# W_out read in rows of 2 KB, w1 - w2 in four parts, and a new order for tile 0's output blocks in a one-core FFT filter with a max-out layer

## The chip, the cores and the metric

One core of one Trainium2 chip runs the whole program in one launch. The metric is the device time of one execution in microseconds (us). TensorE does the matmuls and transposes, VectorE, ScalarE and GpSimd the element-wise work, and SyncE (SP) and GpSimd issue the DMAs. GpSimd's DMAs are the ones that turn fp32 in DRAM into bf16 in SBUF on the way.

## The reference

Each of 8 batch elements has 3072 rows of 256 channels. Every channel is filtered in the frequency domain along the rows, and each filtered row then goes through two matrices, a maximum and an output matrix:

```python
X = np.fft.rfft(x, axis=1)
F = (filt_r + 1j * filt_i)[None, :, :]
y = np.fft.irfft(X * F, n=3072, axis=1)      # 8 x 3072 x 256
h1 = y @ w1                                   # 256 -> 1024
h2 = y @ w2                                   # 256 -> 1024
out = np.maximum(h1, h2) @ w_out              # 1024 -> 256, fp32
```

## The kernel before

**The transform.** 3072 is split into 96 x 32, and the transform is done as matmuls with bf16 tables: 96-point stages (`f1` or `s1` forward, `s4` inverse), 32-point stages with twiddles (`s2` forward, `s3` inverse), and `product` with the filter between them. Between the stages the data has to change its layout. Batch element 0 changes it by transposes on the chip (`s1t`, `t1`, `s3t`, `t2`), the others through two scratch tensors in DRAM: `ad` after the forward 96-point stage, read back as `bt`, and `zd` after the inverse 32-point stage, read back as `zr`. Element 1 goes through `f1`, whose 16 blocks write `ad` in pairs (SP), and `f1_read`, which reads `bt` in two halves (SP). From element 2 on, `load_xf` brings two halves of x into one of three XF buffers (SP), `fold` forms their sum and difference (GpSimd), and `s1` follows.

**The max-out layer.** The maximum is rewritten: max(h1, h2) = relu(y (w1 - w2)) + y w2. With Wd = w1 - w2, Wo = w_out and M = w2 w_out, a row's output is relu(y Wd) Wo + y M. The work goes over 64 tiles of 384 rows, 8 to a batch element. `s4(tt)` makes the transposed y of a tile. `moe_h(tt, j)` gives the j-th of eight blocks of 128 hidden columns: two matmuls into a tile `ph` of the PSUM pool `ps` (six slots), and a relu into `gt` on VectorE or ScalarE. `moe_o(tt, k0, k1)` runs matmuls k0 to k1 of the tile's 30: three output blocks c of 128 rows, each a sum of ten matmuls, eight with Wo and two with M. Blocks are numbered q = 3 tt + c, and two of them share one of the two buffers `po` of the pool `pso`; after the second, VectorE copies the pair to `ot`, and GpSimd issues their two writes to DRAM.

**The order.** It is written out by hand; the engines keep it, and only semaphores let one wait for another. After the opening (tables, element 0's transform, the weights), a loop runs over the tiles in steps, eight to a tile and 64 to a batch element:

```python
for j in range(8):
    step = 8 * i + j
    if tt < 8 * B:
        moe_h(tt, j)
    for fn, a in mid.get((b, step), ()):
        fn(*a)
    if tt > 0:
        n = 3 if j in (3, 7) else 4
        moe_o(tt - 1, k, k + n)
        k += n
    for fn, a in todo.get((b, step), ()):
        fn(*a)
    if j == (4 if i < 7 else 6) and tt + 1 < 8 * B:
        s4(tt + 1)
```

So tile 0's output blocks run during tile 1, from step 8 on. `plan` puts other work at a step: the rest of element 0 (`t2`), element 1's `f1` blocks and `f1_read` (`plan_f1`), and for each later element the loads, folds and "visits" (`plan_f2`). A visit is one sixth of the 32-point stages; visit 0 of element 1, the first to use `bt`, stands at step 24.

**The weights.** `load_w` brings w1 and w2 as fp32 into one tile `WS`, in two halves of 512 hidden columns each (four DMAs of SP, lines 281 and 282). `prep_wd` (line 292, GpSimd) subtracts one half. `cast_w2` (line 285, VectorE) makes `w2b`, the bf16 w2, in four pieces. `prep_t` transposes it (line 299) and ScalarE copies it to `w2T`; `prep_m` (line 306) multiplies it with Wo into M. `load_wo` (line 288) brings w_out with one DMA of GpSimd. On GpSimd's queue the opening ends with two loads of x for element 1, `prep_wd(0)`, `load_wo`, a last load of x, `prep_wd(1)` and `table_ct`. `spin` issues matmuls whose results are not used.

Of the kernel before, what the change touches and what calls it, by code (L numbers as in the profile page):

```python
# [8 lines left out]
FP32 = mybir.dt.float32  # L9
BF16 = mybir.dt.bfloat16  # L10
AF = mybir.ActivationFunctionType
OP = mybir.AluOpType
# [3 lines left out]
D = 256  # L16
# [10 lines left out]
def kernel(  # L27
# [15 lines left out]
    V, S, G, TE = nc.vector, nc.scalar, nc.gpsimd, nc.tensor  # L43
# [8 lines left out]
    Wd = const.tile([128, 2, HID], BF16)  # L52
    Wo = const.tile([128, 8, D], BF16)
# [5 lines left out]
    w2b = const.tile([128, 2, HID], BF16)  # L59
# [9 lines left out]
    pso = ctx.enter_context(tc.tile_pool(name="pso", bufs=2, space=bass.MemoryType.PSUM))  # L69
# [8 lines left out]
    def x_tile(b, c):  # L78
        if c % 2 == 0:
            xb[b] = xpool.tile([128, 8, D], BF16, tag="xb", name="xb")  # L80
        return xb[b][:, 4 * (c % 2):4 * (c % 2) + 4]

    def load_x(b, c, n):
        for k in range(c, c + n):
            xb[b, k] = x_tile(b, k)[0:NP]
        src = x[b].rearrange("(p m) d -> p m d", m=NM)
        m0 = 4 * (c % 2)
        G.dma_start(out=xb[b][0:NP, m0:m0 + 4 * n], in_=src[:, 4 * c:4 * c + 4 * n, :])  # L88
# [98 lines left out]
    def table_ct():  # L187
        G.memset(CT, 0.0)
        for g in range(2):
            G.tensor_copy(CT[64 * g:64 * g + 48, :, 0:48].rearrange("p s (u r) -> p s u r", r=2),  # L190
                          C1[0:48].rearrange("p (u s r) -> p s u r", s=2, r=2))
# [85 lines left out]
    w1f, w2f = WS[:, 0:2], WS[:, 2:4]  # L277
# [4 lines left out]
        nc.sync.dma_start(out=w2f[:, :, js], in_=moe_w2.rearrange("(c p) j -> p c j", p=128)[:, :, js])  # L282

    def cast_w2(h, c):
        V.tensor_copy(w2b[:, c, 512 * h:512 * h + 512], w2f[:, c, 512 * h:512 * h + 512])

    def load_wo():
        G.dma_start(out=Wo, in_=moe_w_out.rearrange("(c p) j -> p c j", p=128))

    def prep_wd(h, engine):  # L290
        js = slice(512 * h, 512 * h + 512)
        engine.tensor_tensor(Wd[:, :, js], w1f[:, :, js], w2f[:, :, js], OP.subtract)  # L292

    def prep_t(jp):
        pt = ps.tile([128, 4, D], BF16, tag="ps", name="pt")
# [126 lines left out]
    def s4(tt):  # L422
        b, i = divmod(tt, 8)
        y_ = ypool.tile([128, 2, 384], BF16, tag="yt", name="y_")
        for dc in range(2):
            py = ps.tile([128, 4, NP], FP32, tag="ps", name="py")
            for m in range(4):
                TE.matmul(py[:, m], zr[b][:, 4 * i + m, 128 * dc:128 * dc + 128], G1, start=True, stop=True)  # L428
            o_ = y_[:, dc].rearrange("p (t m) -> p t m", m=4)
            i_ = py.rearrange("p m t -> p t m")  # L430
            if dc == 0:
                S.activation(o_, i_, AF.Copy, scale=1.0 / 1536.0)
            else:
                V.tensor_scalar(o_, i_, 1.0 / 1536.0, None, OP.mult)
        yt[tt] = y_
# [18 lines left out]
    po = {}  # L454
    ot = {}

    def out_block(tt, c):
        b, i = divmod(tt, 8)
        dst = out[b * N:(b + 1) * N].rearrange("(c p i m) d -> c i p (m d)", c=3, p=32, i=8)[c, i]
        E = G if tt < 8 * B - 2 else nc.sync  # L460
        E.dma_start(out=dst, in_=ot[tt // 2][:, 3 * (tt % 2) + c])  # L461

    def moe_o(tt, k0, k1):
        y_, g_ = yt[tt], gt[tt]
        for k in range(k0, k1):
            c, e = divmod(k, 10)
            n = (e + 2) % 10 if tt == 0 else e
            q = 3 * tt + c
            blk = slice(128 * c, 128 * c + 128)
            if e == 0 and (q % 2 == 0 or q == 24 * B - 1):  # L470
                po[0] = pso.tile([128, 2, D], FP32, tag="po", name="po")
            p_ = po[0][:, q % 2]
            if n < 2:
                TE.matmul(p_, y_[:, n, blk], M[:, n], start=(e == 0), stop=(e == 9))  # L474
            else:
                TE.matmul(p_, g_[:, n - 2, blk], Wo[:, n - 2], start=(e == 0), stop=(e == 9))  # L476
            if e == 9 and q >= 24 * B - 2:
                e = q % 6
                if q % 2 == 0:
                    S.activation(ot[tt // 2][:, e], p_, AF.Copy)  # L480
                else:
                    V.tensor_copy(ot[tt // 2][:, e], p_)
                out_block(tt, c)
            elif e == 9 and q % 2 == 1:
                if q % 6 == 1:
                    ot[tt // 2] = opool.tile([128, 6, D], FP32, tag="ot", name="ot")
                e = q % 6
                V.tensor_copy(ot[tt // 2][:, e - 1:e + 1], po[0])  # L488
                for qq in (q - 1, q):
                    out_block(qq // 3, qq % 3)  # L490

# [48 lines left out]
    def t2(c, engines):  # L540
        if c == 0:
            zr[0] = zrpool.tile([96, NM, D], BF16, tag="zr", name="zr")
        n = 4 // len(engines)
        for k, engine in enumerate(engines):
            pr = ps.tile([96, n, D], BF16, tag="ps", name="pr")
            m0 = 4 * c + n * k
            for m in range(n):
                for dc in range(2):
                    TE.transpose(pr[:, m, 128 * dc:128 * dc + 128], zT[:, dc, m0 + m].rearrange("p u q -> p (u q)"),  # L549
                                 I128)  # L550
            if engine is V:
                V.tensor_copy(zr[0][:, m0:m0 + n], pr)  # L552
            else:
                S.activation(zr[0][:, m0:m0 + n], pr, AF.Copy)

    def spin(n):
        for _ in range(n):
            pd = ps.tile([128, 512], FP32, tag="ps", name="pd")
            TE.matmul(pd, W1[:, 0:128], W1, start=True, stop=True)  # L559
# [73 lines left out]
    for c in (2, 4):  # L633
        load_x(1, c, 2)
    prep_wd(0, G)
    load_wo()
    load_x(1, 6, 2)
    prep_wd(1, G)
    table_ct()
    setup.close()  # L640
    apool = ctx.enter_context(tc.tile_pool(name="apool", bufs=3))
# [4 lines left out]
    f1(1, 0, S)  # L646
    spin(1)
    t2(0, (V, S))
    spin(2)
    s4(0)  # L650
    spin(2)


# [2 lines left out]
    def plan(b, step, fn, *a):  # L656
        todo.setdefault((b + step // 64, step % 64), []).append((fn, a))

    def plan_f1(b, nb, steps, read):
        for c, n in zip(range(1, 16), steps):  # L660
            plan(b, n, f1, nb, c, S if c % 2 == 0 else V)
        plan(b, read, f1_read, nb)
# [3 lines left out]
    def plan_f2(b, steps, quads, xs, folds):  # L666
        for n, st in enumerate(steps):
            mid.setdefault((b, st), []).append((visit, (b + 1, n, quads[n])))
        plan(b, steps[3] + 3, z_read, b + 1, 0)
        plan(b, steps[6] + 3, z_read, b + 1, 1)  # L670
        if b + 2 < B:
            for c in range(8):
                plan(b, xs[c], load_xf, b + 2, c)
                plan(b, folds[c], fold, b + 2, c)
            plan(b, steps[-1] + (6 if b else 11), s1_read, b + 2)

    plan(0, 2, t2, 1, (V,))
    for h in range(2):
        for c in range(2):
            plan(0, 3 + 2 * h + c, cast_w2, h, c)  # L680
    plan(0, 5, prep_t, 0)
    plan(0, 7, prep_t, 1)
    plan(0, 8, prep_m)
    for c in range(2, 8):
        plan(0, 8 * (c - 2) + 8, t2, c, (V,))
    plan_f1(0, 1, (0, 1, 1, 3, 4, 4, 5, 6, 6, 7, 8, 10, 11, 11, 12), 13)
    plan_f2(0, (24, 28, 31, 35, 38, 42, 46), ((0,), (1,), (2,), (3,), (4,), (5,), (6, 7)),
            (6, 10, 14, 18, 21, 25, 29, 33), (14, 18, 21, 25, 28, 32, 36, 40))
    for b in range(1, B - 1):
        plan_f2(b, (7, 14, 18, 24, 31, 38, 42) if b > 1 else (14, 18, 24, 30, 34, 39, 42), ((0, 1), (2,), (3,), (4,), (5,), (6,), (7,)),  # L690
                range(-32, 32, 8) if b > 1 else range(-25, 31, 7), range(-22, 42, 8) if b > 1 else range(-15, 41, 7))
# [1 line left out]
    for tt in range(8 * B + 1):  # L693
        b, i = divmod(tt, 8)
        k = 0
# [14 lines that stand above are left out]
# [30 lines left out]
```

## Time and profile before

| | |
|---|---|
| median of 3 runs | 503.8 us (503.66 to 504.18) |
| the profiled execution | 503.8 us, span 502.0 us |
| mean granted TensorE clock | 0.992 |
| busy TensorE / VectorE / ScalarE / GpSimd | 488.4 / 331.9 / 308.3 / 257.5 us |
| two `prep_wd` on GpSimd | 34.90 to 37.26 and 38.65 to 41.01 us |
| W_out, from issue to landing | 9.4 us, issued at 37.19 |
| first matmul with Wo | 46.64 us |
| read of `bt` for element 1, first half | issued at 56.88, 5.8 us to landing |
| first matmul on `bt` (px) | 62.90 us |

Times of single instructions count from the start of the span. A line of the timeline or of the waits gives in brackets the idle time of the engine before an instruction and what ended it. PEld is TensorE's loading of weights, which runs beside its matmuls. In the rows on DMA queues, q0 holds GpSimd's DMAs and q1 those of SP, and megabytes are those written.

### The profile page before, as it was taken

How to read it: one execution, taken by the hardware profiler on the slowest of the kernel's cores; microseconds unless marked ns; L12 is line 12 of the kernel's file. 1: busy time of each engine (PE TensorE's matmuls, PEld its weight loads, DVE VectorE, ACT ScalarE, POOL GpSimd, SP SyncE). 2: the span in 40 equal slices, each digit the busy share in tenths (PEclk: the TensorE clock that was granted, in tenths of full speed). 3: DMA queues.
4: the chain of work that ended last, by engine and by line, in shares of the span. 5: the costliest groups of instructions: out<-in, count | busy, mean ns of one | idle time of the engine just before them, and what ended most of it. 6: DMA issues, size and time to landing. Idle time of an engine off the chain costs nothing.

```text
span 502.0 us, 13079 instructions
## 1 busy us (share of the span) xinstructions
PE 488.4 (97%) x5299; PEld 362.1 (72%) x5303; DVE 331.9 (66%) x518; ACT 308.3 (61%) x629; POOL 257.5 (51%) x338
## 2 busy tenths in 40 slices
PE   8688999999999999999999999999999999999997
PEld 3455777777777777777777777777777777777775
DVE  7876688457865777457765687557765687555553
ACT  6776478647774676557764586647774465544442
POOL 7893569547463864645654855537632221222220
PEclk9989999999999999999999999999999999999999
DMA  7999789995799667986779558896769235411112
GB/s 125 150 252 217 230 229 290 306 274 171 212 268 260 175 204 234 250 229 189 198 244 275 187 177 245 235 239 197 197 181 255 78 111 153 168 65 64 64 64 84
DMA packets 77966, 97.20 MB, mean 194 GB/s; under 512 B 8017, under 2 KB 54354, under 8 KB 77842
## 3 DMA queue, kind: packets, MB, share of 16 engines
q1 hardware_dynamic: 64642, 66.73, 49.6%
q0 software_dynamic: 13264, 29.64, 20.3%
q8 instruction: 41, 0.67, 0.6%
q14 instruction: 19, 0.16, 0.1%
HBM read 53.87 MB, written 47.19 MB: 201 GB/s over the span
## 4 chain that ended last, share of the span: by engine, by line
PE 90%; DMA 5%; POOL 2%; issue 1%; ACT 1%; DVE 0%; SPq 0%; POOLq 0%; DVEq 0%
PE po L476 34%; PE ph L448 33%; PE po L474 8%; PE pz L399 5%; PE py L428 4%; PE pa L349 2%; DMA F<-in_filt_r_dram 2%; PE px L376 2%; DMA Wo<-in_moe_w_out_dram 2%; POOL xb L88 1%; DMA F<-F 1%; PE pr L549 1%; POOL pq L382 0%; PE pt L528 0%; PE pm__1132 L306 0%
## 5 line engine op out<-in xcount | busy, mean ns | idle before, releaser
L476 PE MATMUL po<-Wo,gt 128*128 128x256 bf16 x1536 | 261.0, 273 | 0.2 <-DMA Wo<-in_moe_w_out_dram 0.2
L452 ACT ACTIVATE gt<-ph 128x384 bf16<-128x384 f32 x321 | 157.0, 496 | 147.9 <-PE ph L448 147.3
L461 POOL DMA_DIRECT2D out_dram<-ot x186 | 102.6, 555 | 187.1 <-DVE ot L488 184.4
L476 PEld LDWEIGHTS <-gt 128*128 128x128 bf16 x1536 | 146.6, 98 | 66.1 <-issue 10.3
L450 DVE TENSOR_SCALAR gt<-ph 128x384 bf16<-128x384 f32 x191 | 104.9, 552 | 63.1 <-PE ph L448 59.9
L382 DVE TENSOR_TENSOR pq<-px,F 128x1024 bf16<-128x1024 f32 x91 | 107.0, 1219 | 24.2 <-PE px L376 22.6
L448 PEld LDWEIGHTS <-Wd 128*128 128x128 bf16 x1024 | 96.5, 98 | 12.9 <-POOL Wd L292 1.4
L103 POOL TENSOR_TENSOR xb<-XF 128x512 bf16<-128x512 f32 x48 | 61.2, 1276 | 41.3 <-DMA XF<-in_x_dram 21.2
L488 DVE COPY ot<-po 128x512 f32<-128x512 f32 x95 | 65.1, 685 | 25.3 <-PE po L476 25.0
L104 POOL TENSOR_TENSOR xb<-XF 128x512 bf16<-128x512 f32 x48 | 61.0, 1271 | 0.0
L403 ACT ACTIVATE zt<-pz 128x512 bf16<-128x512 f32 x84 | 45.6, 595 | 11.5 <-PE pz L399 8.4
L353 ACT ACTIVATE at<-pa 128x512 bf16<-128x512 f32 x96 | 51.8, 610 | 1.2 <-PE pa L349 0.8
L428 PE MATMUL py<-G,zr 96*128 96x96 bf16 x512 | 32.7, 206 | 0.2
L428 PEld LDWEIGHTS <-zr 96*128 96x128 bf16 x512 | 29.0, 97 | 2.5 <-DVE zr L552 0.4
L399 PE MATMUL pz<-pq,VP 64*64 64x256 bf16 x336 | 21.9, 281 | 0.0
L376 PE MATMUL px<-bt,U 64*64 64x256 bf16 x384 | 19.8, 278 | 1.2 <-ACT VQ L273 0.7
L399 PE MATMUL pz<-pq,VQ 64*64 64x256 bf16 x336 | 20.9, 269 | 0.0
L349 PE MATMUL pa<-xb,CT 64*64 64x512 bf16 x192 | 19.5, 383 | 0.0
L399 PEld LDWEIGHTS <-VP 64*64 64x64 bf16 x336 | 9.7, 105 | 13.3 <-issue 13.3
L376 PEld LDWEIGHTS <-U 64*64 64x64 bf16 x384 | 10.4, 109 | 3.9 <-issue 3.3
L559 PE MATMUL pd<-W 128*128 128x512 bf16 x30 | 10.5, 462 | 1.7 <-DVE zero L145 1.5
L552 DVE COPY zr<-pr 96x1024 bf16<-96x1024 bf16 (+1 forms) x8 | 5.2, 649 | 8.0 <-PE pr L549 8.0
(429 smaller groups left out, 609.7 us busy)
## 6 DMA issues: line engine op xcount, KB each, us to landing
out_dram<-ot POOLq DMA_DIRECT2D x186, 128.0 KB, 3.3
XF<-in_x_dram SPq DMA_DIRECT2D x96, 192.0 KB, 4.6
ad<-at SPq DMA_DIRECT2D x56, 192.0 KB, 3.3
bt<-ad SPq DMA_DIRECT2D x14, 768.0 KB, 9.1
zd<-zt SPq DMA_DIRECT2D x42, 256.0 KB, 2.7
zr<-zd SPq DMA_DIRECT2D x56, 192.0 KB, 4.8
WS<-in_moe_w_dram SPq DMA_DIRECT2D x4, 512.0 KB, 5.1
xb<-in_x_dram POOLq DMA_DIRECT2D x8, 192.0 KB, 5.8
```

Source lines behind the costliest of these rows:

```text
L103: G.tensor_tensor(t_[:, 0], f[:, 0], f[:, 1], OP.add)
L104: G.tensor_tensor(t_[:, 1], f[:, 0], f[:, 1], OP.subtract)
L353: S.activation(at[:, m0:m0 + 2], pa[g], AF.Copy)
L382: E.tensor_tensor(pq, px.rearrange("p (o i) d -> p o i d", o=1).to_broadcast([128, 2, 2, D]), F[:, :, 2 * v:2 * v + 2, s], OP.mult)
L399: TE.matmul(pz[g][64 * s:64 * s + 64, i], tab[64 * g:64 * g + 64, 2 * v + i, s], pq[s][64 * g:64 * g + 64, q, i], start=(q == 0), stop=(q ...
L428: TE.matmul(py[:, m], zr[b][:, 4 * i + m, 128 * dc:128 * dc + 128], G1, start=True, stop=True)
L448: TE.matmul(ph, Wd[:, dc, 128 * j:128 * j + 128], y_[:, dc], start=(dc == 0), stop=(dc == 1))
L450: V.tensor_scalar(gt[tt][:, j], ph, 0.0, None, OP.max)
L452: S.activation(gt[tt][:, j], ph, AF.Relu)
L461: E.dma_start(out=dst, in_=ot[tt // 2][:, 3 * (tt % 2) + c])
L476: TE.matmul(p_, g_[:, n - 2, blk], Wo[:, n - 2], start=(e == 0), stop=(e == 9))
L488: V.tensor_copy(ot[tt // 2][:, e - 1:e + 1], po[0])
```

## The change

- `load_wo`: hidden rows 256 q + 2 p + r go to partition p, so that each partition reads two neighbouring rows of w_out (2 KB of fp32) at a time, in four pieces instead of eight of 1 KB. Chunk 2 q + r of Wo then holds every second row of a group of 256.
- `prep_wd` and `cast_w2` put the columns of Wd and `w2b` into the same order, reading every second fp32 column and writing 128 neighbouring ones. `prep_wd` works on quarters (256 hidden columns) instead of halves.
- On GpSimd the opening now ends with the two loads of x, quarters 0 and 1, `load_wo`, quarters 2 and 3, the last load of x, `table_ct`.
- Two of the four casts of w2 go into the opening, behind `t2(0)` and behind `s4(0)`; the others move to steps 3 and 4 (before: 3 to 6), the first `prep_t` from step 5 to 3, and `prep_m` from 8 to 9.
- Tile 0's output matmuls follow the list `FIRST`: the eight Wo blocks of c = 0 and of c = 2, then the four M matmuls of these two, then c = 1. Both buffers `po` are open at once for that; q // 2 % 2 picks the buffer.
- The `f1` blocks from c = 9 on, `f1_read`, and the first three `load_xf` of element 2 move to later steps.

```diff
--- before.py
+++ after.py
@@ -282,14 +282,19 @@
         nc.sync.dma_start(out=w2f[:, :, js], in_=moe_w2.rearrange("(c p) j -> p c j", p=128)[:, :, js])
 
     def cast_w2(h, c):
-        V.tensor_copy(w2b[:, c, 512 * h:512 * h + 512], w2f[:, c, 512 * h:512 * h + 512])
+        o_, i_ = w2b[:, c, 512 * h:512 * h + 512], w2f[:, c, 512 * h:512 * h + 512]
+        V.tensor_copy(o_.rearrange("p (q r j) -> p q r j", q=2, r=2),
+                      i_.rearrange("p (q j r) -> p q r j", q=2, r=2))
 
     def load_wo():
-        G.dma_start(out=Wo, in_=moe_w_out.rearrange("(c p) j -> p c j", p=128))
-
-    def prep_wd(h, engine):
-        js = slice(512 * h, 512 * h + 512)
-        engine.tensor_tensor(Wd[:, :, js], w1f[:, :, js], w2f[:, :, js], OP.subtract)
+
+        G.dma_start(out=Wo.rearrange("p (q r) d -> p q (r d)", r=2),
+                    in_=moe_w_out.rearrange("(q p r) d -> p q (r d)", p=128, r=2))
+
+    def prep_wd(q, engine):
+        js = slice(256 * q, 256 * q + 256)
+        a_, b_ = (w[:, :, js].rearrange("p c (j r) -> p c r j", r=2) for w in (w1f, w2f))
+        engine.tensor_tensor(Wd[:, :, js].rearrange("p c (r j) -> p c r j", r=2), a_, b_, OP.subtract)
 
     def prep_t(jp):
         pt = ps.tile([128, 4, D], BF16, tag="ps", name="pt")
@@ -460,16 +465,20 @@
         E = G if tt < 8 * B - 2 else nc.sync
         E.dma_start(out=dst, in_=ot[tt // 2][:, 3 * (tt % 2) + c])
 
+
+    FIRST = ([(c, e) for c in (0, 2) for e in range(8)] + [(c, e) for c in (0, 2) for e in (8, 9)]
+             + [(1, e) for e in range(10)])
+
     def moe_o(tt, k0, k1):
         y_, g_ = yt[tt], gt[tt]
         for k in range(k0, k1):
-            c, e = divmod(k, 10)
-            n = (e + 2) % 10 if tt == 0 else e
+            c, e = divmod(k, 10) if tt else FIRST[k]
+            n = e if tt else (e + 2) % 10
             q = 3 * tt + c
             blk = slice(128 * c, 128 * c + 128)
             if e == 0 and (q % 2 == 0 or q == 24 * B - 1):
-                po[0] = pso.tile([128, 2, D], FP32, tag="po", name="po")
-            p_ = po[0][:, q % 2]
+                po[q // 2 % 2] = pso.tile([128, 2, D], FP32, tag="po", name="po")
+            p_ = po[q // 2 % 2][:, q % 2]
             if n < 2:
                 TE.matmul(p_, y_[:, n, blk], M[:, n], start=(e == 0), stop=(e == 9))
             else:
@@ -485,7 +494,7 @@
                 if q % 6 == 1:
                     ot[tt // 2] = opool.tile([128, 6, D], FP32, tag="ot", name="ot")
                 e = q % 6
-                V.tensor_copy(ot[tt // 2][:, e - 1:e + 1], po[0])
+                V.tensor_copy(ot[tt // 2][:, e - 1:e + 1], po[q // 2 % 2])
                 for qq in (q - 1, q):
                     out_block(qq // 3, qq % 3)
 
@@ -633,9 +642,11 @@
     for c in (2, 4):
         load_x(1, c, 2)
     prep_wd(0, G)
+    prep_wd(1, G)
     load_wo()
+    prep_wd(2, G)
+    prep_wd(3, G)
     load_x(1, 6, 2)
-    prep_wd(1, G)
     table_ct()
     setup.close()
     apool = ctx.enter_context(tc.tile_pool(name="apool", bufs=3))
@@ -646,8 +657,10 @@
     f1(1, 0, S)
     spin(1)
     t2(0, (V, S))
+    cast_w2(0, 0)
     spin(2)
     s4(0)
+    cast_w2(0, 1)
     spin(2)
 
 
@@ -675,17 +688,16 @@
             plan(b, steps[-1] + (6 if b else 11), s1_read, b + 2)
 
     plan(0, 2, t2, 1, (V,))
-    for h in range(2):
-        for c in range(2):
-            plan(0, 3 + 2 * h + c, cast_w2, h, c)
-    plan(0, 5, prep_t, 0)
+    for c in range(2):
+        plan(0, 3 + c, cast_w2, 1, c)
+    plan(0, 3, prep_t, 0)
     plan(0, 7, prep_t, 1)
-    plan(0, 8, prep_m)
+    plan(0, 9, prep_m)
     for c in range(2, 8):
         plan(0, 8 * (c - 2) + 8, t2, c, (V,))
-    plan_f1(0, 1, (0, 1, 1, 3, 4, 4, 5, 6, 6, 7, 8, 10, 11, 11, 12), 13)
+    plan_f1(0, 1, (0, 1, 1, 3, 4, 4, 5, 6, 7, 8, 9, 11, 11, 12, 13), 14)
     plan_f2(0, (24, 28, 31, 35, 38, 42, 46), ((0,), (1,), (2,), (3,), (4,), (5,), (6, 7)),
-            (6, 10, 14, 18, 21, 25, 29, 33), (14, 18, 21, 25, 28, 32, 36, 40))
+            (9, 11, 16, 18, 21, 25, 29, 33), (14, 18, 21, 25, 28, 32, 36, 40))
     for b in range(1, B - 1):
         plan_f2(b, (7, 14, 18, 24, 31, 38, 42) if b > 1 else (14, 18, 24, 30, 34, 39, 42), ((0, 1), (2,), (3,), (4,), (5,), (6,), (7,)),
                 range(-32, 32, 8) if b > 1 else range(-25, 31, 7), range(-22, 42, 8) if b > 1 else range(-15, 41, 7))
```

## The prediction

> **What bounds the kernel now.** I read the page first, then the waits of TensorE, then the opening (35 to 63 us) engine by engine. The page's engine lines:
>
> ```profile
> span 502.0 us, 13079 instructions
> PE 488.4 (97%) x5299; PEld 362.1 (72%) x5303; DVE 331.9 (66%) x518; ACT 308.3 (61%) x629; POOL 257.5 (51%) x338
> ```
>
> TensorE bounds it, and the change leaves its instruction list the same length, so only TensorE's idle time can be won. After 47 us its view of waits holds one entry, 0.2 us. What the change can reach lies between 37 and 50 us:
>
> ```profile
> PE pt L299 <- DVE w2b L285: 0.7, 1, 0.7
> PE ph L448 <- POOL Wd L292: 0.7, 1, 0.7
> PE po L476 <- DMA Wo<-in_moe_w_out_dram: 0.2, 1, 0.2
> ```
>
> The ends of matmuls are modelled, so I count from start to start instead. In these lines of the timeline a 512-column matmul takes 0.22 us, a 384-column pair 0.33, eight transposes 0.44, eight py matmuls 0.34, a 256-column matmul 0.11:
>
> ```profile
> 41.07 0.50 PE L448 MATMUL ph<-y__984,Wd 128*128 128x384 bf16 x2 [0.67 <-POOL Wd L292]
> 45.35 0.56 PE L299 MATMUL pt<-I,w2b 128*128 128x128 bf16 x7 [0.70 <-DVE w2b L285]
> 46.64 0.60 PE L476 MATMUL po<-Wo,gt 128*128 128x256 bf16 x4 [0.18 <-DMA Wo<-in_moe_w_out_dram]
> ```
>
> So lost are 0.83 us for Wd's second half (40.24 to 41.07), 0.18 and 0.80 for the casts of w2 (42.51 to 42.69, 44.55 to 45.35), 0.34 for Wo (46.30 to 46.64): 2.15 us in all. The next thing that TensorE meets is the read of `bt` for batch element 1, which visit 0 needs at step 24 (62.9 us):
>
> ```profile
> SPq L338 <- DMA ad<-at: 2.2, 2, 1.7
> PEld L376 <- DMA bt<-ad: 0.3, 1, 0.3
> ```
>
> The first says that SP waited for the last writes of `ad` before it could issue this read (at 56.88), the second that the weights of px waited for its landing. The read is on time to 0.1 us: px takes 0.34 there, later 0.22. Nothing saved before 62.9 us counts unless this read comes earlier too.
>
> **Part 1: Wd in four parts, W_out behind two.** GpSimd before:
>
> ```profile
> 34.90 2.36 POOL L292 TENSOR_TENSOR Wd<-WS 128x1024 bf16<-128x1024 f32 x1
> 37.19 0.93 POOL L288 DMA_DIRECT2D Wo<-in_moe_w_out_dram  x1
> 38.12 0.52 POOL L88 DMA_DIRECT2D xb<-in_x_dram  x1
> 38.65 2.36 POOL L292 TENSOR_TENSOR Wd<-WS 128x1024 bf16<-128x1024 f32 x1
> ```
>
> Built, the first quarter waits for all four loads of w1 and w2, where the first half waited for two: its strided view spans both halves. The fourth load was issued at 29.36. The SP queue still moved 40 packets in 35 to 36 us and none in 36 to 37, so it landed between 35.3 and 36.3. I take 36.1, a 1.2 us later start. Behind that wait stand the other quarters, the W_out issue, `load_x(1, 6, 2)` and `table_ct`. A quarter has half the elements of a half (1.18 us); the fold, a 128x512 tensor_tensor, takes 1.27. With 1.25: quarters end at 37.35, 38.6, and after the W_out issue (0.5 to 0.93, I take 0.7: half the descriptors) at 40.55 and 41.8. `load_x(1, 6, 2)` issues at 41.8 instead of 38.12. TensorE wants the quarters at 37.5, 38.9, 40.7 and 42.9. The 0.83 us is won, the first and third with little to spare.
>
> **Part 2: casts of w2.** One costs 0.41; if reading every second element halves the rate, 0.68 (the PSUM cast row). The first sits before VectorE's y copy, in an idle 0.97 us; its data is there (second load: 27.63 + 5.1). The second follows y at 37.73, before an `at` cast that starts at 38.36: up to 0.05 us late. VectorE, which runs without a gap from 38.4 to 45.9, loses two casts there, and the transposes of w2 no longer wait: 0.98 us won. Step 3 now holds the first eight transposes; their copy is ScalarE's.
>
> With Wd and w2b there, TensorE meets the six PSUM slots: the second ph after f1(1, 5) needs the slot that VectorE frees at 42.9, and TensorE is there at 42.3. I charge 0.6 in all. f1(1, 10) moves behind the first W_out block (0.22, moved, not saved). So that block could start at 46.64 - 2.15 - 0.22 + 0.6 = 44.9, and from step 9 on TensorE is 1.5 us ahead.
>
> **Part 3: W_out in 2 KB rows.** Its packets shrink from 1024 to 512. The rates of the GpSimd queue, at 37 to 38 us (x, 4 KB written per packet) and 41 to 42 us (W_out, 512 B):
>
> ```profile
> q0 software_dynamic: 62, 0.20, 106.7%
> q0 software_dynamic: 253, 0.13, 104.6%
> ```
>
> Per engine that is 258 ns and 63 ns a packet. A straight line between them gives 91 ns at 1 KB: 32 packets per engine are 2.9 us where 64 took 4.0. Before, W_out landed 9.4 us after its issue, with its last packets at 46 us beside `load_x(1, 6, 2)` issued right behind it; now 3.2 us lie between the two. Issued at 38.6, first data near 40.1 (1.5 after issue, as x showed), landing between 43.3 and 46: I take 44.8, no wait. The bounds stay in the range.
> The Trainium skill ("DMA: Bandwidth & Descriptors", Specifications) puts line rate at transfers of 512 B and more, which these packets are already; by it the longer rows would bring nothing. The trace speaks against it for this queue, 0.13 MB/us against 0.20. What it would do is rival C.
>
> **Part 4: tile 0's blocks meet W_out first; steps moved.** The same 30 matmuls; M is first used by the seventeenth instead of the ninth, so `prep_m` (1.74 us of TensorE) moves from step 8 to 9 and costs nothing. The first copy of outputs comes at step 15 and GpSimd's fold at step 14 ahead of it: output writes are issued some 1 us later than 55.55, nearer to the `bt` read.
> The rows of f1 from c = 9 on come a step later, `f1_read` at step 14, and the first loads of XF at steps 9 and 11. f1(1, 15) is done at 52.9 instead of 53.3: only 0.4 us earlier, while TensorE is 1.5 ahead. From there to px TensorE has 8.4 us of work (54.40 to 62.81 before), so it is ready at 61.3 to 61.4. The data path took 9.6 us (53.3 to 62.9). Its least is VectorE's cast 0.75, an `ad` write 2.1 (its shortest landing), the read 5.8 and 0.1: `bt` at 61.6. But the XF loads that were issued at 46.3 now go at 49.8 to 51.7, so 1.6 MB (three `ad` writes, two sets of XF) stand in front of the read, entering from 50.7 on. At 0.38 MB/us (the w loads at 33 to 34 us) that ends at 55, so the shortest path holds; at 0.25 to 0.29 (53 to 56 us) at 56.3 to 57.1, against 56.8 before, and px comes at 62.2 to 63.2.
>
> **Sum.** The run of the profile took 503.8 us, span 502.0 and 1.8 around it, equal to the median. Of 1.5 us won, the read of `bt` gives back 0.2 to all of it and a little more. I take px at 62.4 instead of 62.9, between the shortest path and the jam: 503.8 - 0.5 = **503.3**, this case by itself 502.5 to 504.1.
>
> **Rivals.** *B, nothing is given back:* the SP queue runs at the rate of the w loads and `bt` lands with TensorE; 1.5 us are kept: 502.3. For it: the queue idles between 47 and 50 now that XF has left. Against: 90% busy at 0.27 MB/us from 53 to 56.
> *C, W_out stays late and the kernel is slower:* if its time goes by bytes or by what else is in the rings, it lands 8 to 9.4 us after the later issue, at 46.6 to 48.0. TensorE stands at its first block from 44.9, f1(1, 15) slips by 1.7 to 3.1 us, and the data path behind it (8.7 to 9.6 us) brings px at 63.3 to 65.6: about +1.6, 505.4. It decides from a landing at about 46.8 on. For it: laggard engines moved W_out's last 100 packets from 44 to 46 us.
> *E, nothing moves:* the jam takes exactly what is won: 503.8.
>
> **Chances.** My case 0.46, B 0.28, C 0.21, E 0.05. A measurement of this kernel can tell about 0.2%, 1.0 us, from no change. A quarter of my case lies below 502.8. Faster 0.28 + 0.11 = 0.39; same 0.35 + 0.05 = 0.40; slower 0.21. The range takes in B's 502.3 less 0.4 for a PSUM wait smaller than charged, and C up to its middle: 501.9 to 505.4.
>
> **What would show it.** Right: no wait of ph for Wd, none of pt for w2b, the first W_out block near 45, the first quarter near 36.1, and a new wait of TensorE for `bt` of about 1 us near 61.4. B: no such wait. C: po waits for Wo by over 1.5 us. Wrong altogether: f1(1, 12) waits for `load_x(1, 6, 2)`, issued 3.7 us later, or TensorE's time after 63 us changes.

## The result, and the profile after

| | before | after |
|---|---|---|
| median (lowest to highest), 10 runs each | 503.82 us (503.13 to 506.41) | 507.35 us (505.8 to 515.0) |
| ratio after / before, 95% interval | | 1.0066 [1.0041, 1.0090] |
| the profiled execution, its span | 503.8, 502.0 us | 506.12, 504.4 us |
| first matmul with Wo | 46.64 us | 46.41 us |
| first matmul of step 24 | 62.48 us | 62.47 us |
| read of `bt` issued | 56.88 us | 59.84 us |
| px | 62.90 us | 65.21 us |

The change made the kernel slower by 0.7%, some 3.5 us, where 0.5 us of gain was forecast. The ratio leaves out the execution of 515.0 us, which is slow, over 1.5% above the fastest of its kernel. The profiled execution, one of the shortest of its ten, shows 2.3 of them (503.8 to 506.12), and px is late by just these 2.3 (62.90 to 65.21). From px to the end of the execution both take 440.9 us, so all of the loss that this profile shows lies ahead of px. A second trace of this kernel, further down, shows where longer executions lose more. The page after:

```profile
span 504.4 us, 13085 instructions
PE 489.5 (97%) x5303; PEld 362.0 (72%) x5303; DVE 334.1 (66%) x518; ACT 309.0 (61%) x629; POOL 258.8 (51%) x340
```

TensorE's three longest entries in the view of waits (us in total, times, longest):

```profile
PE px L381 <- DMA bt<-ad: 2.3, 1, 2.3
PE ph L453 <- DVE gt L455: 0.9, 1, 0.9
PE ph L453 <- POOL Wd L297: 0.9, 3, 0.4
```

The waits of pt for `w2b` and of po for Wo are gone, as meant. In their place stand three short waits for quarters of Wd, one of ph for a relu of VectorE (`gt`), and a long one for `bt`. The opening on GpSimd:

```profile
36.31 3.15 POOL L297 TENSOR_TENSOR Wd<-WS 128x512 bf16<-128x512 f32 x2 [1.90 <-DMA WS<-in_moe_w_dram]
39.40 0.80 POOL L291 DMA_DIRECT2D Wo<-in_moe_w_out_dram  x1
40.22 2.97 POOL L297 TENSOR_TENSOR Wd<-WS 128x512 bf16<-128x512 f32 x2
```

The first quarter waits for the loads until 36.31 (forecast: 36.1), but two quarters take 3.15 and 2.97 us, not 2.5. VectorE's timeline shows where the relu was:

```profile
37.58 0.52 DVE L286 CAST w2b<-WS 128x512 bf16<-128x512 f32 x1
...
41.36 2.12 DVE L286 CAST w2b<-WS 128x512 bf16<-128x512 f32 x1
43.40 0.55 DVE L455 TENSOR_SCALAR gt<-ph 128x384 bf16<-128x384 f32 x1
```

A cast that takes 0.41 us elsewhere holds VectorE for 2.12. It ends at 43.48, 0.3 us after GpSimd's fourth quarter (43.19). The relu behind it should have freed a PSUM slot at 42.9, and TensorE waits for that slot:

```profile
44.00 0.48 PE L453 MATMUL ph<-y__987,Wd 128*128 128x384 bf16 x2 [0.94 <-DVE gt L455]
...
62.47 0.49 PE L453 MATMUL ph<-y__1325,Wd 128*128 128x384 bf16 x2
65.21 0.41 PE L381 MATMUL px<-bt,U 64*64 64x256 bf16 x8 [2.25 <-DMA bt<-ad]
```

Of the 2.15 us of waits that were removed, 0.9 came back at the quarters and 1.1 (42.90 to 44.00) at the relu. With `f1(1, 10)` moved behind the first block, TensorE's lead is 0.0 there and still 0.0 at step 24. Nothing was won that the read of `bt` could give back; the read itself came 3 us later. SP's queue:

```profile
51.54 0.42 SPq L93 DMA_DIRECT2D XF<-in_x_dram  x1
...
53.50 0.35 SPq L337 DMA_DIRECT2D ad<-at  x1
...
55.37 0.43 SPq L97 DMA_DIRECT2D XF<-in_x_dram  x1
55.91 0.35 SPq L337 DMA_DIRECT2D ad<-at  x1
59.84 1.25 SPq L343 DMA_DIRECT2D bt<-ad  x2
```

Eight loads of XF stand close in front of the last write of `ad`. From the issue of that write to the issue of the read, which waits for its landing, pass 3.9 us (55.91 to 59.84); in the kernel before it was 2.6 (54.25 to 56.88). So of the 3 us, 1.7 are the later issue of the write and 1.3 its slower landing. The rows of SP's DMA queue (packets, megabytes, share of the 16 engines) at 51 to 52 us and at 54 to 55 us:

```profile
q1 hardware_dynamic: 3, 0.01, 1.6%
q1 hardware_dynamic: 142, 0.24, 90.0%
```

The queue lay idle where the kernel before had XF moving (0.23 MB at 49 to 50 us), and was full when the last writes of `ad` came.

### The profile page after: what moved, and what is told of

It is laid out like the page before. It is cut to its first block, busy times and chain, and to the rows that moved or that the text cites. A ratio compares the mean times of both kernels' runs of the same rounds, so it can differ in the third digit from the quotient of the medians.

```text
span 504.4 us, 13085 instructions
## 1 busy us (share of the span) xinstructions
PE 489.5 (97%) x5303; PEld 362.0 (72%) x5303; DVE 334.1 (66%) x518; ACT 309.0 (61%) x629; POOL 258.8 (51%) x340
## 4 chain that ended last, share of the span: by engine, by line
PE 88%; DMA 6%; POOL 3%; DVE 1%; SPq 1%; issue 0%; ACT 0%; POOLq 0%
PE po L485 33%; PE ph L453 32%; PE po L483 8%; PE pz L404 5%; PE py L433 4%; PE pa L354 2%; PE px L381 2%; DMA xb<-in_x_dram 2%; DMA WS<-in_moe_w_dram 1%; DMA bt<-ad 1%; DMA F<-in_filt_i_dram 1%; POOL F L117 1%; DMA ad<-at 1%; POOL xb L88 1%; POOL F L120 1%; PE pr L558 0%
## 5 line engine op out<-in xcount | busy, mean ns | idle before, releaser
L354 PEld LDWEIGHTS <-CT 64*64 64x64 bf16 x192 | 8.7, 105 | 2.2 <-ACT gt L457 1.2
```

## The experiments

Two accounts were to be told apart. *The queue account*: the loss is the XF loads, moved by hand from steps 6 and 10 to 9 and 11, in front of the last `ad` write. *The opening account*: the loss is made at 36 to 46 us, by the casts beside GpSimd's subtractions, the slower quarters and the wait for four loads, and is carried on. The expectations speak of a queue theory and, for the casts and quarters, of a port theory. Every ratio is against the kernel before on the same chip.

**The moved steps undone.** The changed kernel with the steps of `f1`, `f1_read` and XF of before:

```diff
-    plan_f1(0, 1, (0, 1, 1, 3, 4, 4, 5, 6, 7, 8, 9, 11, 11, 12, 13), 14)
-            (9, 11, 16, 18, 21, 25, 29, 33), ...
+    plan_f1(0, 1, (0, 1, 1, 3, 4, 4, 5, 6, 6, 7, 8, 10, 11, 11, 12), 13)
+            (6, 10, 14, 18, 21, 25, 29, 33), ...
```

> The changed kernel with f1, f1_read and the XF loads at the steps of before. Queue theory (the loss is that the first XF loads now stand behind f1's eleventh row and in front of its last ad write, so that the read of bt comes 3 us late): the read is issued near 57 us, px waits under 0.5 us, the time is 503.5 to 504.3. Port theory (the loss is the w2 cast that takes 2.12 us beside the Wd quarters, and the quarters at 1.5 us): both stay as they are, the time stays at 506 or above.

Measured: 504.73 us, ratio 1.0014 [0.9994, 1.0033]. The read of `bt` is issued at 57.54, px waits 0.2 us, while the cast still takes 2.12 us and TensorE still waits 1.5 for quarters and 0.9 for the relu. Most of the loss is gone with the opening unmended.

**Only the XF steps undone** (the second of the two lines above).

> The changed kernel with only the XF loads at the steps of before; f1 and f1_read stay late. Queue theory: most of the 2.3 us wait of px goes, since XF no longer fills the queue ahead of the last ad writes; f1(1, 15) is done about 1 us later than before, so px is late by 0.5 to 1.0: 504.3 to 505.0. If f1's later rows are the cause and not the XF loads: px still waits 2 us, 506. Port theory: 506 and above.

Measured: 505.01 us, 1.0023 [0.9999, 1.0046]; `bt` issued at 57.94, px waits 0.2. The last `ad` write is issued at 55.90, as late as in the changed kernel, but the read follows 2.0 us behind it instead of 3.9. So XF makes most of it: with the rows of `f1` and `f1_read` late as well, px runs at 63.70, only 0.4 us later than in the first experiment (63.31).

**The last two casts late**, at steps 5 and 6 of the changed kernel.

```diff
-        plan(0, 3 + c, cast_w2, 1, c)
+        plan(0, 5 + c, cast_w2, 1, c)
```

> The changed kernel with the last two casts of w2 at steps 5 and 6, behind the Wd quarters. Port theory: the cast takes 0.41 us, TensorE's 0.94 us wait for VectorE goes, the first W_out block starts near 45.5 and the time falls by 1 us or more, below 505. Queue theory: TensorE gains that 0.9 us in the opening, but the XF loads and the last ad write still keep the read of bt late; it moves with f1(1, 15) by up to 0.9, so px keeps a wait of 2 to 3 us and the time is 505.2 to 506.1.

Measured: 507.32 us, 1.0069 [1.0044, 1.0095], as the change itself. All four casts take 0.41 to 0.43 us there. The profiled execution (509.53 us) can't price that: in it the loads of w1 and w2 were late, the first quarter began at 38.67 and TensorE waited 3.1 us for it. But in the six executions a cast out of GpSimd's way left the median where it was.

**The moved steps alone**, put into the kernel before (the first diff the other way round).

> The kernel before, with nothing changed but f1, f1_read and the XF loads, which take the steps of the changed kernel. Queue theory: the read of bt is issued near 60 us and px waits 2 to 3 us: 506 to 507. Port theory: no cast and no quarter is touched, so the time stays within 0.3 of 503.8.

Measured: 508.22 us, 1.0077 [1.0054, 1.0100]. This kernel has the opening of before (halves in 2.36 us, casts in 0.41), and yet its waits and its SP queue show the same loss:

```profile
PE px L376 <- DMA bt<-ad: 2.4, 1, 2.4
```
```profile
56.16 0.36 SPq L332 DMA_DIRECT2D ad<-at  x1
60.81 1.25 SPq L338 DMA_DIRECT2D bt<-ad  x2
```

From the last `ad` write's issue to that of the read pass 4.7 us. px runs at 65.64, 2.7 us later than before; another 1.7 us of this execution (508.24 us) are lost behind px, by TensorE's clock, as the second trace of the changed kernel explains below. Two lines of step numbers, without the rest of the change, make px as late as the whole change does.

**Two loads instead of four for the first quarter.** The first experiment's kernel, with w1 and w2 laid out by halves, so that the strided view of a quarter spans one half only.

```diff
-    WS = zrpool.tile([128, 4, HID], FP32, tag="zr", name="WS")
+    WS = zrpool.tile([128, 2, 4, 512], FP32, tag="zr", name="WS")
...
+        ws = WS[:, q // 2, :, 256 * (q % 2):256 * (q % 2) + 256].rearrange("p c (j r) -> p c r j", r=2)
+        a_, b_ = ws[:, 0:2], ws[:, 2:4]
```

> As the run with the steps of before (e1), but w1 and w2 lie in one tile by halves, so that the first two Wd quarters wait for the first two loads alone. If the wait for all four loads costs time: quarter 0 starts when the x loads are issued (33.2 to 34.9 us) instead of 36.5, TensorE's 1.5 us of waits for Wd go, the time falls from 504.7 to 503.6 to 504.2, and its scatter to that of the kernel before (503.4 to 505). If the read of bt sets the end whatever the opening does: 504.5 to 505 as in e1.

Measured: 504.72 us (502.95 to 509.62), 1.0033 [0.9997, 1.0068]; six runs lie at 502.95 to 505.25 and four at 508.2 to 509.6. The wait for the loads is gone. The profiled execution is one of the four long ones (508.23 us); GpSimd and VectorE in it:

```profile
34.89 2.96 POOL L297 TENSOR_TENSOR Wd<-WS 128x512 bf16<-128x512 f32 x2
37.79 0.80 POOL L290 DMA_DIRECT2D Wo<-in_moe_w_out_dram  x1
38.60 2.93 POOL L297 TENSOR_TENSOR Wd<-WS 128x512 bf16<-128x512 f32 x2
```
```profile
36.42 5.41 DVE L285 CAST w2b<-WS 128x512 bf16<-128x512 f32 x1
41.75 0.55 DVE L439 TENSOR_SCALAR y__987<-py 128x384 bf16<-128x384 f32 x1
```

The cast begins at the end of the first quarter and ends 0.3 us after the fourth: it was held for all of GpSimd's work, the issue of the DMA included. The `y` copy of tile 0 is behind it, and the first ph waits 4.2 us for `y`. Right behind that wait TensorE's granted clock is 0.50 from 42.7 to 46.1 us.

**The casts on ScalarE**, in the first experiment's kernel, each as two instructions.

```diff
-        V.tensor_copy(o_.rearrange("p (q r j) -> p q r j", q=2, r=2),
-                      i_.rearrange("p (q j r) -> p q r j", q=2, r=2))
+        for q in range(2):
+            js = slice(256 * q, 256 * q + 256)
+            S.activation(o_[:, js].rearrange("p (r j) -> p r j", r=2), i_[:, js].rearrange("p (j r) -> p r j", r=2), AF.Copy)
```

> As e1, with the four casts of w2 on ScalarE (two instructions each). Port theory: no VectorE cast stands behind a running subtraction of GpSimd, so the 2.1 us cast and TensorE's 0.9 us wait for VectorE go, ScalarE takes about 0.45 us an instruction, the Wd quarters lose the 0.1 to 0.2 us that the first took longer; the time falls by 0.3 to 0.9. Rival (the cast was slow because of its strided read): ScalarE is slow on it too, above 1 us an instruction, and TensorE waits for it.

Measured: 504.40 us, 1.0025 [1.0002, 1.0048]. Six of ten runs lie at 504.17 to 504.50. The waits for casts, relu and quarters are gone from the profiled execution (505.81 us), and a new one stands there: po waits 1.9 us for W_out, which landed at 48.6. The quarters still take 1.50 to 1.52 us with no cast beside them, so that is the price of reading every second column.

**The 2 KB rows alone**, in the kernel before, with the row order that they need in `prep_wd` and `cast_w2`. w1 and w2 lie by halves in their tile, as in the fifth experiment, and a half is subtracted in two instructions.

```diff
-        G.dma_start(out=Wo, in_=moe_w_out.rearrange("(c p) j -> p c j", p=128))
+        G.dma_start(out=Wo.rearrange("p (q r) d -> p q (r d)", r=2),
+                    in_=moe_w_out.rearrange("(q p r) d -> p q (r d)", p=128, r=2))
...
```

> The kernel before with the 2 KB rows and the column order that they need, the subtraction of a half as two strided 128x512 instructions, w1 and w2 by halves in their tile, and nothing else moved. If reading every second fp32 column costs GpSimd: 1.5 us for each of the four instead of 1.2, the second half 1.3 us later, and the first w2 cast held up by it. If the 1.5 us came from the casts beside them: 1.2. W_out: if its time goes by rows, landing 6.5 to 7 us after its issue, else 9. The time: 503.6 to 504.6, since the read of bt follows f1 as before.

Measured: 504.99 us, 1.0023 [1.0010, 1.0035]. W_out lands 9.1 us after its issue; with rows of 1 KB it took 9.4. The subtractions (four of 128x512) take 1.50 to 1.68 us each, and ph waits 1.3 us for Wd. The rows bring W_out hardly earlier, and the order that they force on the columns costs.

**The order `FIRST` alone**, with `prep_m` at step 9, in the kernel before.

```diff
-            c, e = divmod(k, 10)
-            n = (e + 2) % 10 if tt == 0 else e
+            c, e = divmod(k, 10) if tt else FIRST[k]
+            n = e if tt else (e + 2) % 10
...
-    plan(0, 8, prep_m)
+    plan(0, 9, prep_m)
```

> The kernel before with tile 0's blocks in the order of the changed kernel and prep_m at step 9, nothing else. Nothing waits for M or for a PSUM buffer that did not before: within 0.3 us of before, 503.6 to 504.2. If the first output writes, 1 us later, get in the way of the read of bt: px waits 0.5 us or more, 504.5.

Measured: 503.89 us, 0.9996 [0.9985, 1.0008]. Neutral.

**Two casts in the opening, on VectorE**, in the kernel before, behind `t2(0)` and `s4(0)`.

```diff
+    cast_w2(0, 0)
...
+    cast_w2(0, 1)
...
-    for h in range(2):
-        for c in range(2):
-            plan(0, 3 + 2 * h + c, cast_w2, h, c)
+    for c in range(2):
+        plan(0, 5 + c, cast_w2, 1, c)
```

> The kernel before with the first two casts of w2 in the opening as in the changed kernel, and nothing else moved; the casts read neighbouring columns. Port theory (a two-port VectorE cast and a GpSimd instruction hold the same SBUF ports, and the later one waits until GpSimd's queue has a gap): the first cast meets the first subtraction (34.9 to 37.3 us) and takes 1 to 5 us instead of 0.41; y and TensorE wait behind it, 1 to 4 us longer: 504.5 to 508, with a wide scatter. Stride theory (only the strided cast is slow): 0.41 us, the time within 0.3 of 503.9, and the two casts gone from tile 0 save up to 0.5.

Measured: 509.31 us in four runs (505.96 to 509.79), 1.0088 [1.0063, 1.0114]. VectorE and GpSimd in the profiled execution:

```profile
38.07 1.37 DVE L285 CAST w2b<-WS 128x512 bf16<-128x512 f32 x1
```
```profile
36.50 2.66 POOL L292 TENSOR_TENSOR Wd<-WS 128x1024 bf16<-128x1024 f32 x1 [1.18 <-DMA WS<-in_moe_w_dram]
...
42.82 2.34 POOL L292 TENSOR_TENSOR Wd<-WS 128x1024 bf16<-128x1024 f32 x1 [2.25 <-DMA WS<-in_moe_w_dram]
```

The cast again ends 0.3 us after the subtraction beside it. But that explains 1 us; the second half waited 2.25 us for its loads, ph 4.3 us for Wd in all, and `bt` was issued at 61.82. Behind the longest of these waits (2.8 us) the granted clock is 0.50 from 45.3 to 48.7 us. Why the loads of w1 and w2 are late there isn't shown.

**A mend: casts on ScalarE, contiguous columns.** The kernel before, with rows of 1 KB, two casts in the opening and two at steps 2 and 4 (all on ScalarE), the first `prep_t` at step 3, the second half of Wd as two contiguous quarters, and the last load of x behind them.

```diff
-        V.tensor_copy(w2b[:, c, 512 * h:512 * h + 512], w2f[:, c, 512 * h:512 * h + 512])
+        S.activation(w2b[:, c, 512 * h:512 * h + 512], w2f[:, c, 512 * h:512 * h + 512], AF.Copy)
...
-    prep_wd(0, G)
+    prep_wd(0, 512, G)
     load_wo()
+    prep_wd(512, 256, G)
+    prep_wd(768, 256, G)
     load_x(1, 6, 2)
-    prep_wd(1, G)
```

> A version of its own from the kernel before, W_out in 1 KB rows: casts of w2 on ScalarE, two in the opening and two at steps 2 and 4, the second half of Wd in two quarters ahead of the last load of x. If port and queue theories hold: no wait for a cast, none for Wd, contiguous quarters at 1.2 us; TensorE is 1 to 1.8 us ahead at the first W_out block, the XF loads and f1 move with it, and the read of bt too: 502.2 to 503.2. If W_out's landing or the read of bt gives it back: 503.6 to 504.2.

Measured: 503.18 us in 12 runs (502.18 to 506.95), 0.9994 [0.9976, 1.0012]. It has the lowest median of all, but can't be told from the kernel before. Its only lasting wait, and its quarters on GpSimd:

```profile
PE po L476 <- DMA Wo<-in_moe_w_out_dram: 0.8, 1, 0.8
```
```profile
37.49 2.50 POOL L292 TENSOR_TENSOR Wd<-WS 128x512 bf16<-128x512 f32 x2
```

A contiguous quarter takes 1.25 us, and the casts on ScalarE take 0.62 each, in the middle of a quarter or not. With `bt` issued at 56.02, px runs at 62.03, 0.9 us earlier than before, and the execution is 0.9 us shorter (502.93). So the link between px and the end holds for a gain too. In the other six runs the gain isn't there.

**The last load of x behind the second subtraction**, in the kernel before (`load_x(1, 6, 2)` and `prep_wd(1, G)` change places).

> The kernel before with the last load of x issued behind the second subtraction, 2.4 us later, and nothing else. If that load was what kept W_out (and not the length of its rows): W_out lands 6.5 to 7.5 us after its issue, with 1 KB rows. If the rows: 9 to 9.5 us as before. The time stays within 0.5 of 503.9 in both.

Measured: 504.15 us, 1.0003 [0.9993, 1.0013]. W_out lands 8.3 us after its issue, at 45.2. That lies between the two landings that were expected, so it doesn't tell the load of x from the rows. This part is free and brings nothing by itself.

**The change, mended**: the first experiment's kernel with w1 and w2 by halves and the casts on ScalarE (the fifth and sixth diffs together). 2 KB rows and strided quarters stay.

> The changed kernel with all three causes taken out: f1, f1_read and XF at the steps of before, w1 and w2 by halves in their tile so that the first quarter waits for two loads, casts on ScalarE. 2 KB rows and strided quarters stay. Port, queue and wait theories together: no wait above 0.5 us for Wd or for a cast, px on time, 503.0 to 504.0, little scatter. If W_out's landing sets it: po waits for Wo by 1 us or more, 504.2 and above.

Measured: 504.08 us, 0.9996 [0.9983, 1.0009]. No wait for a cast, a relu or a quarter is left; po waits 2.3 us for W_out, which lands 10.1 us after its issue, at 46.9.

**The moved steps in the mended kernel** (the first diff the other way round).

> The changed kernel with casts on ScalarE and w1 and w2 by halves in their tile; the moved steps stay. If the moved steps make 2 to 3 us and the opening makes the rest and the scatter: 506 to 507.3, px waiting 2 to 3 us for bt, its runs within 2 us of each other. If the opening makes most of it: 504.0 to 505.

Measured: 506.92 us, 1.0056 [1.0035, 1.0076]. Against the kernel above that is 2.8 us, and 3.0 by the two ratios. Its waits name the place again:

```profile
PE px L382 <- DMA bt<-ad: 1.9, 1, 1.9
```

px runs at 65.62, against 63.23 in the kernel above. So at px the steps cost 1.9 us with a disturbed opening (65.21 against 63.31 in the first experiment), 2.7 with the opening of before, and 2.4 with a mended one.

**The opening's two casts on ScalarE**, otherwise as the ninth experiment.

```diff
-    cast_w2(0, 0)
+    cast_w2(0, 0, True)
...
-    cast_w2(0, 1)
+    cast_w2(0, 1, True)
```

> As e9 (the kernel before with two casts of w2 in the opening), with these two on ScalarE in the same places. Port theory: 0.62 us each, no wait of TensorE behind them beyond 0.3 us, 503.6 to 504.4 where e9 had 505.96 to 509.79. If the late landing of the w loads, which e9's profile shows, belongs to casts in the opening whatever the engine: 506 and above.

Measured: 504.76 us, 1.0007 [0.9993, 1.0021], against 1.0088 with the same casts at the same places on VectorE. Each takes 0.62 us, and the loads of w1 and w2 are in time.

**The changed kernel again**, one execution.

> The changed kernel once more, for a second profile. Its time is 505.8 to 510. If the scatter comes from the opening, the first cast or the first quarter is held differently than in the first profile (a cast of 4 to 5 us, or the first quarter starting after 37.5 us), and the wait for bt is the same 2 to 3 us; if it comes from the moved steps, the opening looks as before and the wait for bt is longer or shorter.

Measured: 509.26 us. The four casts (0.41, 0.52, 2.11, 0.41 us), the first quarter (36.15) and the wait of px (2.3) are as in the first profile. New is a wait of po for W_out, 1.5 us: it landed at 47.9 instead of 46.1, and the `bt` read is issued 1.5 us later for it (61.36). The scatter of the changed kernel is thus partly W_out's, as rival C described it, but on top of the queue's loss. The two spans differ by 3.1 us, and px is later by 1.5 (66.71 against 65.21). The other half lies behind px: from there to the end this execution takes 442.55 us instead of 440.9. The view by stretches, here for 68 to 70 us of this trace and of the first one, gives each engine's busy time and, as its last three figures, TensorE's granted clock, the DMA share and GB/s:

```profile
68.00:70.00 2.00, 2.00 (x14) 1.54 (x13) 2.00 (x3) 0.47 (x1) 0.00 (x0) 0.50 1.12 325
```
```profile
68.00:70.00 2.00, 2.00 (x39) 1.50 (x36) 1.08 (x3) 1.49 (x4) 0.00 (x0) 1.00 1.05 193
```

In this trace the clock is 0.50 from 67.3 to 70.7 us, and 3.4 us at half speed cost 1.7. Every profile has a stretch at 0.50 between 22 and 35 us, but later than that the kernel before has none. The same 3.4 us stand in five other profiles, each time right behind a wait of TensorE: in the fourth experiment behind the 2.4 us of px, in the third, fifth, ninth and last ones behind waits of 3.1, 4.2, 2.8 and 2.0 us in the opening. Behind the 2.25 us of px in the first profile and the 2.3 us of po in the twelfth experiment the clock stays at 1.00, so the length of the wait alone doesn't decide it. Executions without a trace have only their mean clock: five of the changed kernel's ten, at 507.18 to 515.0 us, have 0.990 or less, the other five, at 505.8 to 507.71 us, 0.992 or more. It fits that a part of the median's loss beyond the 2.3 us is clock, but where these executions lost it isn't shown.

**W_out earlier still**: the mended kernel of rows of 1 KB, with the x load of blocks 4 and 5 behind W_out and the first subtraction.

```diff
-    for c in (2, 4):
-        load_x(1, c, 2)
+    load_x(1, 2, 2)
+    load_wo()
     prep_wd(0, 512, G)
-    load_wo()
+    load_x(1, 4, 2)
```

> As e10 (casts on ScalarE, Wd in a half and two quarters, 1 KB rows), with W_out ahead of the first subtraction and of the load of x blocks 4 and 5. If W_out's landing is set by what stands in front of it in GpSimd's queue: it lands near 42 to 43.5 us instead of 45.7, the 0.8 us wait for it goes, 502.0 to 502.8; f1(1, 8) may wait up to 1 us for its x blocks, then 502.8 to 503.5. If its landing is set by the traffic of 44 to 46 us: 45 to 46 us again, 503.

Measured: 505.50 us, 1.0009 [0.9988, 1.0029]. W_out is issued at 34.68 and lands at 42.8, no matmul waits for it, and the wait stands elsewhere (`pa` are the matmuls of `f1` on x):

```profile
PE pa L324 <- DMA xb<-in_x_dram: 2.0, 1, 2.0
```

In the other seventeen profiles it lands between 45.2 and 48.7, issued between 36.5 and 41.8. Two things differ here, a load of x less in front of it and an issue 1.9 us earlier than the mend's; which of them moved the landing isn't separated. Either way the time was only shifted to x, and behind this wait the granted clock is 0.50 from 46.1 to 49.5 us.

## Why the prediction was wrong

*The sign, Part 4.* The mechanism was named: XF in front of the `ad` writes delays the read of `bt`. Its size was wrong: the term "gives back 0.2 to all of 1.5 us and a little more" measured 2.3 (px at 65.21 instead of 62.2 to 63.2). Two things in that step failed. It took TensorE to be 1.5 us ahead, and the lead to pull the moved steps forward: the last `f1` block done at 52.9, the first four XF loads issued at 49.8 to 51.7. Block 15 was done at 54.4, and those loads were issued from 51.54 on, the next four up to 55.80. And it gave the queue too little time for the 1.6 MB in front of the read: they were to enter from 50.7 on and be through by 57.1 at the latest. SP's queue took from 52 to 59 us for 1.62 MB, 0.23 MB/us, below the lowest rate in the sum (0.25):

```profile
q1 hardware_dynamic: 965, 1.62, 81.3%
```

Even with everything 1.5 us earlier the read would go out at 58.3 and px run at 63.7 (estimates, from 59.84 and 65.21), both later than in the kernel before. So the lead alone wouldn't have made the gain; but no run has the moved steps with a lead, and how the loss divides between the two isn't measured. The fourth and thirteenth experiments show the price without a lead by itself: px later by 2.7 and 2.4 us.

*The lead, Part 2.* A cast was priced 0.41 or 0.68 us; the one beside the third and fourth quarters took 2.12, and the charge of 0.6 us for PSUM slots was 1.1. Wherever a trace shows a VectorE cast held beside subtractions (the changed kernel and its repetition, the first, second, fifth, seventh and ninth experiments), the cast ends 0.3 us after the end of one; on ScalarE none was held. The Trainium skill ("SBUF — State Buffer", Who interferes with whom) says that VectorE's two-port forms of copy and cast share a port pair with GpSimd, that the later of the two is blocked entirely until the other is done, and that ScalarE waits for nobody. The traces agree in kind, though no view says in which form a cast runs, and show the other direction too: the subtraction after the cast that got in at 37.82 took 1.67 us instead of 1.50. They go further than one instruction: the cast of 2.12 us was passed over once and that of 5.41 us twice, while others got in at the first end. That rule spoke against the change, and the prediction didn't weigh it.

*Part 1.* The wait for four loads and the start of the first quarter (36.1, measured 36.31) were right. A quarter was priced 1.25 us from contiguous rows; strided it takes 1.50, contiguous 1.25. With the first and third quarter "little to spare", 0.25 us each was enough: 0.9 us of waits came back.

*Part 3.* W_out landed at 46.1, not at 44.8. The rate was forecast about right; what failed is the step from the rate to the landing. GpSimd's queue at 44 to 45 us of the changed kernel and at 41 to 42 us with the rows alone, both with packets of W_out's 1 KB only:

```profile
q0 software_dynamic: 167, 0.17, 101.9%
```
```profile
q0 software_dynamic: 184, 0.19, 118.5%
```

Counted as in Part 3 these are 96 and 87 ns a packet, where the straight line gave 91, and 0.17 and 0.19 MB/us against 0.13. Yet alone the rows moved the landing only from 9.4 us after the issue to 9.1, and kernels with the shorter rows show 8.1 to 10.1. The Trainium skill ("DMA: Bandwidth & Descriptors", Specifications) puts line rate at transfers of 512 B and more. These rates differ from it for this queue, as the prediction argued, though the landing comes out as if longer rows brought nothing. No matmul waited in the profiled run only because TensorE was late as well.

*Rivals.* B (502.3) fell with the lead. C had the sign and, in the repetition, its own wait of 1.5 us, but isn't what makes the loss. "Nothing moves" fell. Of what would have made the forecast wrong altogether, `f1(1, 12)` waiting for x didn't come. TensorE's time after px is the same in the first profile, but 1.6 us longer in the repetition: the prediction had no term for a wait that is followed by a lower clock.

*Right:* the order `FIRST` with `prep_m` at step 9 costs nothing (0.9996), the waits of pt for `w2b` and of po for Wo go, and what is saved before px counts only if `bt` comes earlier, as the mend's profiled run shows with 0.9 us on both.

*Open:* why the loads of w1 and w2 land late in some executions (the third and ninth experiments); why a held cast gets in after one subtraction in one place and not in another; why the granted clock falls behind some waits of TensorE of 2.0 to 2.4 us and not behind others; what the longer executions without a trace lost, and where.

## What to carry to other kernels

A step number written out by hand fixes an order on a DMA queue. Before moving loads, look at which small write they come to stand in front of, and what is read back from it; price the move with no lead won elsewhere, as a case of its own. A wait of TensorE of two us or more can cost more than itself: look at the granted clock behind it. When casts are spread into idle gaps of VectorE, look at what GpSimd does in that gap: on ScalarE they cost 0.62 us instead of 0.41, but they don't wait.

## What the runs showed of the hardware

A VectorE cast of 128x512 from fp32 to bf16, 0.41 us by itself, lasted up to 5.41 us beside GpSimd's fp32 subtractions (1.05, 1.37 and 2.12 in other traces), and ended 0.3 us after the end of one each time. In six of eighteen profiles TensorE's granted clock was, later than 35 us, 0.50 for 3.4 us right behind a wait of 2.0 to 4.2 us; where that lay behind px, the rest took 1.6 and 1.7 us longer; behind other waits of 1.9 to 2.3 us it stayed at 1.00. On GpSimd, a 128x512 subtraction that reads every second fp32 column takes 1.50 us, contiguous 1.25. W_out's landing hardly followed its issue: issues from 36.5 to 41.8 landed between 45.2 and 48.7, with rows of 1 KB and of 2 KB alike: the four issues from 39.4 on (all with rows of 2 KB) after 6.5 to 6.9 us, the earlier ones after 7.8 to 10.1.
